# Reordering the front of a fused attention and feed-forward kernel: early masks, later transposes, shared weighing of V, one AV head behind each score tile

## The chip, the cores and the metric

The kernel runs on one core of one Trainium2 chip. Times are device microseconds (us) of one execution. Most executions of a kernel agree within 0.3%; the change concerns about 1%, so the comparisons below use several runs and a 95% interval. A run carries its mean granted TensorE clock (1.0 is full speed). Runs called slow (over 1.5% above the fastest of the same kernel) are left out of the ratios; the medians are over all runs, slow ones too.

## The reference

Batch 8, 8 heads, 576 positions, head size 64: forgetting attention (the scores carry a decay that is the difference of two running sums of log f), followed by a feed-forward layer with exact GELU over the 512 joined head columns.

```python
scores = scale * np.matmul(q, k.transpose(0, 1, 3, 2))
cum    = np.cumsum(np.log(np.clip(f, 0.0001, 1.0)), axis=-1)
scores = np.where(causal, -1e9, scores + cum[:, :, :, None] - cum[:, :, None, :])
attn   = softmax(scores)                      # row maximum taken off, 1e-9 in the sum
x      = (attn @ v).transpose(0, 2, 1, 3).reshape(4608, 512)
h      = x @ w_in                             # 512 x 2048
out    = (0.5 * h * (1 + erf(h / sqrt(2)))) @ w_out
```

## The kernel before

Eight batches go through the same pipeline: attention of batch b is woven into the feed-forward matmuls of batch b-1. For the first batch there is nothing to weave into. That stretch, written out by hand, is the *front*, the first 25 us, and the change touches only it.

The decay is split: the factor that belongs to a query cancels in the softmax, and the factor of a key, exp(-cum), is multiplied into V and into a 65th column of V that yields the sum. This multiplication is the *weighing*. Four *pairs* of heads are numbered 0 to 3; `scores(0, i, t)` is one of four score tiles of pair i with its exponential on ScalarE; `attend_head(i, h)` is an *AV head*, 15 matmuls and a normalization on VectorE.

```python
def weigh_v(b, i, eng=nc.gpsimd):             # V of one pair times exp(-cum)
    ...
    eng.tensor_tensor(vw_of[b][:, hs, :, 0:D], v_sb[:, hs, :, :],
                      w.unsqueeze(3).to_broadcast([P, 2, NBLK, D]), Alu.mult)
    eng.tensor_copy(vw_of[b][:, hs, :, D], w)

def transposes_first(b, i, which, pool, tag): # q or k of one pair on TensorE
    ...                                       # 12 transposes into ps, then ONE copy:
    op = nc.scalar.copy if b == i == which == 0 else nc.vector.tensor_copy
    op((qT, kT)[which][i]..., ps...)

def first_attention():
    ...                                       # pairs 0 and 1
    scores(0, 1, 0)
    transposes(2, m_psum, "m")
    scores(0, 1, 1)
    scores(0, 1, 2)
    transposes(3, m_psum, "m")
    scores(0, 1, 3)
    weigh_v(0, 0, nc.vector)
    gate = x_pool.tile([P, 1], FP32, tag="gate", name="gate")
    nc.gpsimd.tensor_copy(gate[D:P], v_sb[D:P, 0, 4, 0:1])   # holds GpSimd until V is there
    load_w_in(0)
    weigh_v(0, 1)
    load_w_in(1)
    weigh_v(0, 2)
    weigh_v(0, 3)
    ...                                       # loads of the next batch
    scores(0, 2, 0); scores(0, 2, 1); scores(0, 2, 2); scores(0, 2, 3)
    attend_head(0, 0)
    scores(0, 3, 0)
    attend_head(0, 1)
    scores(0, 3, 1)
    ...                                       # the other heads, three to_xT
    gemm1_begin(0, both)                      # first feed-forward matmuls
```

Ahead of this, GpSimd's order of loads and masks: q and k of pairs 0 and 1, an identity, q and k of pair 2, V (issued by SyncE), then two masks (`key_of`, `after`), each a memset and a select on GpSimd, then q and k of pair 3. In the traces each engine works through its own list in the order written here (the kernel has a manual schedule). So whatever stands in front of an instruction in its engine's list delays it, needed or not.

The softmax here doesn't subtract the row's maximum and nothing guards it: scores larger than these inputs give would overflow.

## Time and profile before

| | before |
|---|---|
| median of the runs with the changed kernel | 345.62 us (345.02 to 345.96, 4 runs) |
| span of the profiled run, mean clock | 343.4 us, 0.999 |
| first score exponential | 8.43 us |
| AV head (0,0) starts | 17.36 us |
| first feed-forward matmul ("front's end") | 24.50 us |

These three moments are the yardstick for the front, and the prediction shows the chain of waits that leads to them. Two more lines are needed later. The first is from the table of stretches (window; length; busy us and instructions of TensorE, its weight loads, VectorE, ScalarE, GpSimd; granted clock; DMA share; GB/s), for the sparsest stretch of the front. The second is from GpSimd's timeline: the select that makes a mask.

```profile
15.04:18.46 3.42, 2.30 (x49) 1.56 (x47) 1.47 (x5) 3.34 (x5) 3.05 (x6) 1.00 0.58 84
```

```profile
7.13 0.40 POOL L141 TENSOR_SCALAR_AFFINE_SELECT after<-after 64x256 bf16<-64x256 bf16 x1
```

TensorE is busy 2.30 of 3.42 us (67%) where ScalarE paces, and the clock stays at 1.00. The select takes 0.40 us; VectorE beside it copies keys out of PSUM until 7.26 and a mask from 7.29 on.

### The profile page before, as it was taken

The numbers are of one execution on the slowest core, as the hardware profiler recorded it, in microseconds if no ns is written. First come the engines' busy times: TensorE is split into PE (matmuls) and PEld (weight loads), VectorE is DVE, ScalarE is ACT, GpSimd is POOL, SyncE is SP. The second block draws the span as 40 slices with busy tenths as digits, with TensorE's granted clock in tenths as the row PEclk, the third lists the DMA queues.
The fourth block names the chain that finished last, engine by engine and source line by source line (L and its number), as shares of the span: only waits on it lengthen the run. The fifth ranks groups of instructions, "written<-read, shape, count | busy, mean of one in ns | idle before, by whom it ended". The sixth has DMA issues, their size and how long they took to land.

```text
span 343.4 us, 7895 instructions
## 1 busy us (share of the span) xinstructions
PE 328.6 (96%) x3182; PEld 174.7 (51%) x3227; DVE 187.0 (54%) x424; ACT 212.3 (62%) x296; POOL 124.2 (36%) x256
## 2 busy tenths in 40 slices
PE   7799999999999999999999999999999999999995
PEld 3574555445554456545654565446544654444443
DVE  5660355933467935796479646974597542020011
ACT  5986786773644787368746874687468755504600
POOL 8390672228328034543445243714261430000000
PEclk9999999999999999999999999999999999999999
DMA  8999999989993999578945896499900230011013
GB/s 117 178 176 194 201 166 153 170 158 148 237 184 102 139 192 188 82 101 165 211 121 73 141 212 139 71 160 198 169 31 2 65 88 31 2 61 61 0 38 87
DMA packets 99924, 43.03 MB, mean 125 GB/s; under 512 B 78704, under 2 KB 95344, under 8 KB 99888
## 3 DMA queue, kind: packets, MB, share of 16 engines
q1 hardware_dynamic: 82592, 28.37, 41.4%
q0 software_dynamic: 16896, 13.63, 27.2%
q8 instruction: 25, 0.41, 0.5%
q10 hardware_dynamic: 400, 0.52, 0.4%
q14 instruction: 11, 0.09, 0.1%
HBM read 36.85 MB, written 9.44 MB: 135 GB/s over the span
## 4 chain that ended last, share of the span: by engine, by line
PE 89%; issue 2%; POOL 2%; DVE 2%; ACT 2%; DMA 2%; POOLq 0%; ACTq 0%; DVEq 0%
PE ps L375 36%; PE ps L466 25%; PE o L320 9%; PE ps L408 8%; PE s L289 7%; PE ps L501 2%; ACT e L299 2%; DMA k<-in_k_dram 2%; PE ps_x L353 1%; DVE x L334 1%; POOL q L107 1%; PE ps_f L206 1%; POOL k L107 1%; DVE r L333 0%; DVE xT L356 0%
## 5 line engine op out<-in xcount | busy, mean ns | idle before, releaser
L392 ACT ACTIVATE g<-ps 128x512 bf16<-128x512 f32 x144 | 85.3, 597 | 81.1 <-PE ps L375 81.1
L299 ACT ACTIVATE e<-s 128x896 bf16<-128x896 f32 (+2 forms) x128 | 101.2, 836 | 28.5 <-PE s L289 26.8
L375 PE MATMUL ps<-xT,w_in_sb 128*128 128x512 bf16 x497 | 111.4, 379 | 0.8
L466 PE MATMUL ps<-w_out_sb,g 64*128 64x512 bf16 (+1 forms) x731 | 103.0, 376 | 0.8 <-issue 0.8
L375 PEld LDWEIGHTS <-w_in_sb 128*128 128x128 bf16 x576 | 56.0, 98 | 67.5 <-issue 1.8
L301 POOL TENSOR_SCALAR_AFFINE_SELECT e<-e 128x256 bf16<-128x256 bf16 (+1 forms) x135 | 49.2, 383 | 98.9 <-ACT e L299 98.6
L466 PEld LDWEIGHTS <-g 64*128 64x128 bf16 (+1 forms) x756 | 41.5, 94 | 40.4 <-issue 11.9
L244 DVE COPY qT<-tq 64x288 bf16<-64x288 bf16 x96 | 48.7, 507 | 1.4
L289 PE MATMUL s<-qT,kT 64*128 64x320 bf16 (+4 forms) x384 | 45.8, 276 | 3.6 <-ACT e L299 2.7
L260 POOL TENSOR_TENSOR vw<-v_sb,wT 128x640 bf16<-128x640 f32 x31 | 39.6, 1278 | 23.5 <-DMA v_sb<-in_v_dram 23.3
L320 PE MATMUL o<-vw,e 128*128 128x65 bf16 x960 | 36.8, 194 | 3.5 <-issue 2.4
L474 DVE COPY ot<-ps 128x512 f32<-128x512 f32 x26 | 17.9, 689 | 37.1 <-PE ps L466 35.2
L320 PEld LDWEIGHTS <-e 128*128 128x128 bf16 x960 | 34.8, 98 | 5.3 <-PE ps_x L353 0.3
L244 DVE COPY kT<-tk 64x288 bf16<-64x288 bf16 x96 | 33.0, 343 | 1.6
L334 DVE TENSOR_TENSOR x<-o,r 128x320 bf16<-128x320 f32 x64 | 31.4, 491 | 2.4 <-DVE r L333 0.2
L417 DVE COPY ot<-ps 128x512 f32<-128x512 f32 (+2 forms) x9 | 5.7, 632 | 48.8 <-PE ps L408 31.9
L289 PEld LDWEIGHTS <-kT 64*128 64x128 bf16 x384 | 19.5, 94 | 23.2 <-issue 9.7
L408 PE MATMUL ps<-w_out_sb,g 128*128 128x512 bf16 (+2 forms) x142 | 27.9, 355 | 0.1
L333 DVE RECIPROCAL r<-o 128x5 f32<-128x5 f32 x64 | 12.1, 189 | 27.6 <-PE o L320 27.5
L408 PEld LDWEIGHTS <-g 128*128 128x128 bf16 x144 | 13.5, 98 | 14.5
L476 DVE TENSOR_TENSOR ot<-ot,ps 128x512 f32<-128x512 f32 x26 | 17.9, 687 | 1.5
L365 POOL COPY tails<-xT 128x256 bf16<-128x256 bf16 x8 | 3.2, 399 | 31.3 <-DVE xT L356 31.3
(64 smaller groups left out, 158.1 us busy)
## 6 DMA issues: line engine op xcount, KB each, us to landing
out_dram<-ot SPq DMA_DIRECT2D x32, 256.0 KB, 2.3
v_sb<-in_v_dram SPq DMA_DIRECT2D x24, 256.0 KB, 5.3
q<-in_q_dram POOLq DMA_DIRECT2D x6, 576.0 KB, 6.1
k<-in_k_dram POOLq DMA_DIRECT2D x6, 576.0 KB, 8.2
v_sb<-in_v_dram SPq DMA_DIRECT2D x22, 128.0 KB, 5.1
w_in_sb<-in_moe_w_in_dram POOLq DMA_DIRECT2D x4, 512.0 KB, 6.7
w_out_sb<-in_moe_w_out_dram POOLq DMA_DIRECT2D x4, 512.0 KB, 8.4
q<-in_q_dram POOLq DMA_DIRECT2D x4, 144.0 KB, 4.6
```

The source lines that it names most:

```text
L244: nc.vector.tensor_copy(rows[:, odd], src[odd * D : (odd + 1) * D, 2 * i + h].rearrange("d j p -> d p j"),)
L260: eng.tensor_tensor(vw_of[b][:, hs, :, 0:D], v_sb[:, hs, :, :], w.unsqueeze(3).to_broadcast([P, 2, NBLK, D]), Alu.mult,)
L289: nc.tensor.matmul(to, *ab, start=half < 0, stop=half == 1 or not masked)
L299: nc.scalar.activation(et[:, :, z:c], st[:, :, z:c], Act.Exp, scale=scale)
L301: nc.gpsimd.affine_select(out=et[:, :, c0 + z : c0 + P], in_=et[:, :, c0 + z : c0 + P], compare_op=Alu.is_ge, fill=0.0, base=z, pattern=[[ ...
L320: nc.tensor.matmul(o[:, m, :], e_of[b, i, t][:, h, c : c + P], vw_of[b][:, 2 * i + h, n, :], start=(n == 0), stop=(n == m),)
L334: nc.vector.tensor_tensor(x_of[b, i][:, :, h, :], o[:, :, 0:D], r.unsqueeze(2).to_broadcast([P, NBLK, D]), Alu.mult,)
L375: nc.tensor.matmul(ps, w_in_sb[:, kt, ffb * P : (ffb + 1) * P], src[:, kt, 0:TC], start=(kt == 0), stop=(kt == n_dm - 1),)
L392: nc.scalar.activation(g_of[c][ffb], ps, Act.Gelu)
L408: nc.tensor.matmul(pss[ts][:, c0:c1], g_of[c][kt][:, ts * P : (ts + 1) * P], w_out_sb[:, kt, c0:c1], start=(kt == 0), stop=(kt == n_ff - 1),)
L466: nc.tensor.matmul(banks[r], g_of[c][kt][rows, ts * P : (ts + 1) * P], w_out_sb[rows, kt, :], start=kt == (steps.index("r") if r else 0), ...
L474: nc.vector.tensor_copy(ot, banks[1])
```

## The change

The intent: have the masks ready earlier, take the last key load out of the way of ScalarE's exponentials, relieve GpSimd of half the weighing, and spread the AV heads so that fewer are left when the exponentials end.

```diff
@@ order of loads and masks
+    warm = ...; nc.vector.memset(warm, 0.0)                 # moved up
     load_qk_tokens(0, 0, 2); load_qk_tokens(0, 2, 4); make_identity(nc, ident_bf)
-    load_qk_tokens(0, 4, 6)
-    nc.gpsimd.memset(v_sb[:, :, 0, 0:1], 0.0)
-    load_v(0, 0, 4)
     for t, op, fill in ((key_of, ...), (after, ...)):
-        nc.gpsimd.memset(t[0:D], 0.0)
+        nc.vector.memset(t[0:D], 0.0)
         nc.gpsimd.affine_select(...)
+    nc.gpsimd.memset(v_sb[:, :, 0, 0:1], 0.0)
+    load_v(0, 0, 4)
+    load_qk_tokens(0, 4, 6)
@@ first_attention
     transposes(0, o_psum, "o")
+    nc.scalar.activation(wk, cum, Act.Exp, ...)             # was ahead of transposes(0)
     ...
+    nc.vector.tensor_copy(vw(0)[:, :, :, D], ...)           # one cast in place of four
     scores(0, 1, 2)
-    transposes(3, m_psum, "m")
     scores(0, 1, 3)
-    weigh_v(0, 0, nc.vector)
-    nc.gpsimd.tensor_copy(gate[D:P], v_sb[D:P, 0, 4, 0:1])
+    nc.gpsimd.tensor_copy(gate, v_sb[:, 0, 3, 0:1])
     load_w_in(0); weigh_v(0, 1); load_w_in(1)
-    weigh_v(0, 2)
     weigh_v(0, 3)
+    scores(0, 2, 0)
+    scores(0, 2, 1)
+    transposes(3, m_psum, "m")
+    weigh_v(0, 0, nc.vector)
+    scores(0, 2, 2)
+    attend_head(0, 0)
+    scores(0, 2, 3)
+    attend_head(0, 1)
+    weigh_v(0, 2, nc.vector)
     ...                                  # loads of the next batch
-    scores(0, 2, 0) ... scores(0, 2, 3)  # and heads (0,0), (0,1), ... behind them
+    scores(0, 3, 0); attend_head(1, 0); scores(0, 3, 1); attend_head(1, 1)
+    scores(0, 3, 2); attend_head(2, 0); scores(0, 3, 3); ...
```

More of the change, by code (lines that the diff above doesn't have):

```diff
@@ L122, in load_v @@
             )
+    warm = consts.tile([P, TC], BF16)
+    nc.vector.memset(warm, 0.0)
     f_sb = consts.tile([BH, S], FP32)
@@ L180 @@
     wk = f_sb
-    warm = consts.tile([P, TC], BF16)
-    nc.vector.memset(warm, 0.0)
     nc.vector.memset(ones, 1.0)
@@ L188 @@
     nc.vector.tensor_tensor_scan(cum, ones, lf, 0.0, Alu.mult, Alu.add)
-    nc.scalar.activation(wk, cum, Act.Exp, bias=cum[:, S // 2 : S // 2 + 1], scale=-1.0)
     def warm_up(n):
@@ L251, with vw, weigh_v @@
     vw_of = {}
-    def weigh_v(b, i, eng=nc.gpsimd):
+    def vw(b):
         if b not in vw_of:
             vw_of[b] = v_pool.tile([P, H, NBLK, D + 1], BF16, tag="vw", name=f"vw{b}")
+        return vw_of[b]
+    def weigh_v(b, i, eng=nc.gpsimd):
         hs = slice(2 * i, 2 * i + 2)
@@ L260, in weigh_v @@
         eng.tensor_tensor(
-            vw_of[b][:, hs, :, 0:D],
+            vw(b)[:, hs, :, 0:D],
             v_sb[:, hs, :, :],
@@ L265, in weigh_v @@
         )
-        eng.tensor_copy(vw_of[b][:, hs, :, D], w)
+        if b:
+            eng.tensor_copy(vw(b)[:, hs, :, D], w)
     e_of = {}
@@ L539, in first_attention @@
         transposes(0, o_psum, "o")
+        nc.scalar.activation(
+            wk, cum, Act.Exp, bias=cum[:, S // 2 : S // 2 + 1], scale=-1.0
+        )
         nc.vector.tensor_copy(key_of[D:P], key_of[0:D])
@@ L554, in first_attention @@
         nc.vector.tensor_copy(wT[D:P, 4, :], psw[D:P, 4, :])
+        nc.vector.tensor_copy(
+            vw(0)[:, :, :, D], wT[:, :, 0:H].rearrange("p n h -> p h n")
+        )
         scores(0, 1, 0)
@@ L575, in first_attention @@
         load_qk_tokens(1, 4, 8)
-        scores(0, 2, 0)
-        scores(0, 2, 1)
-        scores(0, 2, 2)
-        scores(0, 2, 3)
-        attend_head(0, 0)
         scores(0, 3, 0)
-        attend_head(0, 1)
+        attend_head(1, 0)
         scores(0, 3, 1)
-        attend_head(1, 0)
+        attend_head(1, 1)
         scores(0, 3, 2)
-        attend_head(1, 1)
+        attend_head(2, 0)
         scores(0, 3, 3)
         to_xT(0, 0, nc.vector.tensor_copy)
-        attend_head(2, 0)
         attend_head(2, 1)
```

## The prediction

> **What bounds the kernel now.** First the page: span, busy shares, the chain that ended last.
>
> ```profile
> span 343.4 us, 7895 instructions
> PE 328.6 (96%) x3182; PEld 174.7 (51%) x3227; DVE 187.0 (54%) x424; ACT 212.3 (62%) x296; POOL 124.2 (36%) x256
> PE 89%; issue 2%; POOL 2%; DVE 2%; ACT 2%; DMA 2%; POOLq 0%; ACTq 0%; DVEq 0%
> ```
>
> TensorE makes up 89% of the chain. The non-TensorE shares sit mostly at the start, the only place the change touches, so I read the chain for the first 30 us (start, length, what; the gaps are mine):
>
> ```profile
> 8.15 5.64 DMA k<-in_k_dram
> 13.84 0.56 PE ps_f L206 x12
> 14.39 0.35 PE s L289 x6
> 14.76 2.22 ACT e L299 x3
> ...
> 17.03 0.40 PE s L289 x6
> 17.43 0.58 PE o L320 x15
> 18.01 0.47 PE s L289 x12
> 18.47 0.58 PE o L320 x15
> ...
> 23.97 0.47 PE o L320 x15
> 24.45 0.05 issue
> 24.50 0.81 PE ps L375 x3
> ```
>
> Three stretches. Up to 13.8 us the last key load decides, because its 24 transposes stand in TensorE's order in front of a score tile. From 14.8 to 17.0 ScalarE's exponentials (L299) pace. From 17.0 to 24.5 TensorE alternates score tiles (0.30 to 0.47 us) and AV heads (15 matmuls, 0.58 us) nearly without a gap. The first feed-forward matmul (L375) stands at 24.50; call this the front's end. After it the chain is matmul after matmul to about 38 us and nothing in it waits for a DMA, so I take a shift of the front's end to pass 1:1 into the total.
>
> Then VectorE's timeline and GpSimd's (start, length, instruction, idle before):
>
> ```profile
> 13.43 0.76 DVE L213 COPY qT<-ps_f 128x576 bf16<-128x576 bf16 x1
> 14.43 0.76 DVE L213 COPY kT<-ps_f 128x576 bf16<-128x576 bf16 x1 [0.25 <-PE ps_f L206]
> 15.11 0.82 DVE L260 TENSOR_TENSOR vw<-v_sb,wT 128x640 bf16<-128x640 f32 x1
> 18.04 0.20 DVE L333 RECIPROCAL r<-o 128x5 f32<-128x5 f32 x1 [1.92 <-PE o L320]
> ```
>
> ```profile
> 14.88 0.19 POOL L563 COPY gate<-v_sb 64x1 f32<-64x1 f32 x1 [4.94 <-DMA v_sb<-in_v_dram]
> 16.21 1.27 POOL L260 TENSOR_TENSOR vw<-v_sb,wT 128x640 bf16<-128x640 f32 x1
> 18.41 1.29 POOL L260 TENSOR_TENSOR vw<-v_sb,wT 128x640 bf16<-128x640 f32 x1
> 19.80 1.28 POOL L260 TENSOR_TENSOR vw<-v_sb,wT 128x640 bf16<-128x640 f32 x1
> ```
>
> The reader is to see that the first weighing of V (VectorE) is finished at 15.9, long before the first AV head asks for it at 17.4: now nobody waits for it. Finally two VectorE timelines from later, for the same kind of copy (SBUF to SBUF): four of them alone, and four while GpSimd weighs.
>
> ```profile
> 61.52 1.45 DVE L244 COPY kT<-tk 64x288 bf16<-64x288 bf16 x4
> ```
>
> ```profile
> 142.74 5.04 DVE L244 COPY qT<-tq 64x288 bf16<-64x288 bf16 x4
> ```
>
> **What the Trainium skill says.** "GPSIMD Engine Reference", section 8 (Key points): GpSimd shares its SBUF interfaces with VectorE, with contention for VectorE instructions in a 2-port mode or with two SBUF inputs. The trace agrees strongly for the copies: alone, four take 1.45 us together (0.32 each in the single records); the second row's three that lie under a GpSimd weighing of 1.27 take 1.45 each, as 14 do in the whole trace, and the weighing isn't slowed. For a VectorE weighing (two SBUF inputs) no overlap occurs in this trace. The same page, 4.1 (Engine selection), puts GpSimd at about 2x slower for two-input elementwise work; here 1.28 against 0.82 us, 1.56x. "ScalarE: Activation LUTs", What ACT_TABLE_LOAD costs: about 1283 ns a load plus a drain; the trace has 1.28 us and no drain between (Ln ends 4.74, load 4.76 to 6.05, Exp at 6.16). "TensorE: Matmul & The Clock Gate", What's actually happening: an idle window of about 3.4 us halves the clock; here it stays at 1.00 through the sparse stretch 15.9 to 17.4.
>
> **The change, part by part.**
>
> *Masks early.* Two GpSimd memsets (about 0.25 us each exposed) go to VectorE, which has the room before the f load lands at 3.55. GpSimd's selects are done near 5.5 instead of 7.5. But the score tile waits for the copies of both masks to the upper partitions on VectorE, which stand behind the kT copy (6.50 to 7.26) and end at 7.93 either way. Gain: nothing. The q/k loads of pair 2 are issued 0.9 us later (5.6 and 6.25) and, with about 4.9 us to landing, arrive by 11.3; their transposes come near 11.6 to 12.0. Just in time.
>
> *Exponential of the decay after the qT copy.* The instruction order shows that the table load moves with it: qT copy 6.06 to 6.68, load to 7.96, Exp (0.78) to 8.75, less 0.1 overlap: the first score exponential starts at 8.67 instead of 8.43. Cost 0.24 us; ScalarE paces from here, so it carries.
>
> *Last pair's transposes behind two more score tiles.* This removes the stall at 13.8: ScalarE idled 0.61 there. Stepping on with the recorded spacing of back-to-back exponentials (0.81, 0.69, 0.80, 0.60 for a pair's four tiles) and the gap that stays around pair 2's transposes, exponential (1,3) runs 14.28 to 14.98. Score tile (2,1) takes the freed buffer at 15.03; the transposes follow at 15.33 (0.30 after, as now after the other 6-matmul tile).
>
> *Weighing of pair 0.* In VectorE's new order it still stands behind these transposes' two copies. qT copy at 15.92 (0.59 after the first transpose, as twice before), kT 16.59, weighing 17.27, with 0.82 us to 18.09. AV head (0,0) stands in TensorE's order behind score tile (2,2), which is done near 16.4, and ahead of tile (2,3). So it waits until 18.14, against 17.36 now, and ScalarE starves behind it from about 17.4. The wait for the key load has become a longer wait for a weighing.
>
> *Is the weighing alone on the SBUF?* GpSimd's gate now looks at a V piece landing near 13.5 instead of 14.9, so w_in's first piece is issued at 14.0, weighing (0,1) runs 14.8 to 16.1, issue to 16.9, weighing (0,3) 16.95 to 18.2. It covers VectorE's start at 17.27. If that is blocked as the copies are, it ends near 18.2 + 0.75 = 18.95 and the head starts at 19.0.
>
> *From the first head to the front's end.* TensorE's work there: 8 heads, score tiles (2,3) to (3,3), 3 groups of transposes of x. Adding the recorded lengths in the new order: 8 x 0.58 + 0.33 + 0.47 + 0.30 + 0.38 + 0.33 + 3 x 0.30 = 7.35 us. Now it is 24.50 - 17.36 = 7.14 without tile (2,3), including about 0.2 of gaps. VectorE keeps up: each head costs it 0.71, the weighing (0,2) of 0.82 after head (0,1) ends 0.7 us before it is used. One head fewer after the last exponential helps nothing where TensorE is the limit. So the front ends at 18.14 + 7.35 = 25.5 (alone) or 19.0 + 7.35 = 26.35 (blocked): +1.0 or +1.85 us.
>
> *Casts.* Three GpSimd casts of 0.22 and one on VectorE of 0.29 become one VectorE copy at about 11.3, in idle time: 0 on the path. Loads of w_in and of batch 1's q and k keep their issue times within 1 us (the memset ahead of them now waits for VectorE's weighing (0,2), ending at 21.2 to 22.1; it stands at 21.16 now) and have over 1 us of slack against a later front.
>
> Sum: +0.24 (Exp), -0.6 (stall removed), then a new wait, for a net +1.0 to +1.85 us. Weighting blocked at two to one: 345.62 + 1.6 = about 347.2.
>
> **Rivals.**
> A: the intended gain. Without the wait for the weighing, ScalarE would end its 16 tiles near 21.5 (8.67 + four pairs of 2.9 + gaps) and, with one head fewer behind, the front would end 1.35 us earlier: 344.3. For it: the stall at 13.8 is real. Against it: the orders of VectorE and TensorE, which fix the wait; and TensorE's 7.35 us after that head.
> B: weighing alone on the SBUF, because GpSimd's second weighing starts later than VectorE's or VectorE isn't blocked with two inputs: 346.6. For it: V's second half may land later now that w_in competes with it. Against it: the 1.45 us copies.
> C: pair 2's loads land late (V is now issued ahead of them): another 0.3 to 0.8 us of ScalarE idle near 12. But most of it falls in front of the same wait: up to 348.
> D: TensorE's lull (16.4 to 19.0, 2.6 us) trips the clock gate: a few us at half rate, +1 to +2 us. Against: under the 3.4 us window.
>
> **Range and chances.** Both main branches are slower; A's level needs an error in the orders that I read. Low 345.9 leaves room for half the wait, high 348.4 for C on top of the blocked case. 2% is 6.9 us, five times what is at play in a front of 25 us: faster 0.005, within 0.985, slower 0.01.
>
> **What would show it.** Right: the head (0,0) waiting for VectorE's weighing of V, ScalarE idle over 1.2 us before tile (2,3); that weighing lasting over 1.2 us if blocked, 0.82 if alone; first score exponential at about 8.7; no wait for k; L375's counterpart first at 25.4 to 26.4. Wrong: head (0,0) starting before 17.4, a wait for pair 2's keys over 0.5 us, a granted clock below 1 near 20, or a front shift that the span doesn't repeat.

## The result, and the profile after

The changed kernel takes 348.09 us in the median (347.60 to 348.82, 4 runs) against 345.62. The ratio is 1.0072 [1.0054 to 1.0089]. Within 2%, and slower beyond doubt. The four clocks are 0.988 to 0.995, where the kernel before has 0.999 in its profile. The profiled run is the slowest of the four.

From the page: span, and the clock in 40 slices (in tenths, 9 is full speed).

```profile
span 347.0 us, 7892 instructions
...
PEclk9969999999999999999999999999999999999999
```

The span grew by 347.0 - 343.4 = 3.6 us, and one slice near the front's end has a low clock. The chain of waits through the front (start, length, what; `s` is a score tile, `o` an AV head, `ps` the feed-forward; the line numbers differ by one from the kernel before):

```profile
16.22 0.75 DVE kT L210
16.97 1.24 DVE vw L260
18.20 0.04 issue
18.24 0.98 PE o L321 x15
19.23 0.54 PE s L290 x6
19.77 0.94 PE o L321 x15
...
28.10 0.81 PE ps L376 x3
```

Where the chain before read "ScalarE's exponential, score tile, AV head", two VectorE steps stand: the copy of pair 3's keys, then the weighing of V (`vw`). The head (0,0) starts at 18.24 instead of 17.36, though it uses nothing of pair 3. TensorE's timeline has the wait itself, in brackets:

```profile
18.24 0.98 PE L321 MATMUL o<-vw,e 128*128 128x65 bf16 x15 [2.10 <-DVE vw L260]
```

And the head runs slowly: 0.94 to 0.98 us for the 15 matmuls that took 0.58 before. The front ends at 28.10 instead of 24.50: 3.60 us later, all that the span grew.

VectorE's and GpSimd's timelines give the two weighings and the mask:

```profile
16.88 1.31 DVE L260 TENSOR_TENSOR vw<-v_sb,wT 128x640 bf16<-128x640 f32 x1
```

```profile
4.96 1.45 POOL L138 TENSOR_SCALAR_AFFINE_SELECT after<-after 64x256 bf16<-64x256 bf16 x1
...
6.41 0.68 POOL L107 DMA_DIRECT2D q<-in_q_dram  x1
...
16.21 1.29 POOL L260 TENSOR_TENSOR vw<-v_sb,wT 128x640 bf16<-128x640 f32 x1
```

VectorE's weighing takes 1.31 us instead of 0.82 where GpSimd's of pair 1 overlaps it. The select takes 1.45 us instead of 0.40, because it now lies beside VectorE's running sum (from 4.66, for 1.54 us instead of 1.35), and the q load of pair 2 behind it is issued at 6.41 instead of 4.69.

The table of stretches tells why the heads are slow:

```profile
14.28:17.69 3.41, 1.80 (x48) 1.29 (x43) 2.15 (x3) 2.79 (x4) 2.46 (x4) 1.00 0.68 121
17.69:21.10 3.41, 2.86 (x44) 2.35 (x45) 1.51 (x5) 0.70 (x1) 0.55 (x1) 0.50 1.24 209
21.10:24.52 3.42, 3.42 (x52) 2.41 (x49) 2.42 (x6) 1.73 (x2) 2.85 (x4) 0.50 0.72 118
```

The clock's records stand on a grid of 3.41 us, on which I laid the stretches. In 14.28 to 17.69 TensorE is busy 1.80 us, 53%. In the two stretches that follow the granted clock is 0.50. TensorE's wait for the weighing is 2.1 us (16.16 to 18.24), far less than one stretch; it was enough that 1.53 us of it fell into one. The rest of it, 0.55 us, lies in the next stretch, where TensorE was busy 2.86 us (84%), and the clock stayed at 0.50 for one stretch more.

### The profile page after: what moved, and what is told of

Read it like the earlier page. It is cut to its first block, busy times and chain, and to the rows that moved or that the text cites. A ratio compares the mean times of both kernels' runs of the same rounds, so it can differ in the third digit from the quotient of the medians.

```text
span 347.0 us, 7892 instructions
## 1 busy us (share of the span) xinstructions
PE 330.7 (95%) x3182; PEld 176.1 (51%) x3227; DVE 188.7 (54%) x427; ACT 212.5 (61%) x296; POOL 123.9 (36%) x250
## 4 chain that ended last, share of the span: by engine, by line
PE 91%; ACT 3%; DVE 3%; issue 2%; POOL 0%; ACTq 0%; DVEq 0%
PE ps L376 35%; PE ps L467 25%; PE o L321 9%; PE ps L409 8%; PE s L290 8%; ACT e L300 2%; PE ps L502 2%; PE ps_x L354 1%; PE ps_f L203 1%; PE ps_w L192 1%; DVE x L335 1%; DVE kT L210 0%; ACT L541 0%; DVE vw L260 0%; DVE xT L357 0%
## 5 line engine op out<-in xcount | busy, mean ns | idle before, releaser
L290 PE MATMUL s<-qT,kT 64*128 64x320 bf16 (+4 forms) x384 | 46.7, 280 | 3.7 <-ACT e L300 3.0
L321 PE MATMUL o<-vw,e 128*128 128x65 bf16 x960 | 38.4, 197 | 5.4 <-issue 2.4
L321 PEld LDWEIGHTS <-e 128*128 128x128 bf16 x960 | 36.2, 100 | 7.5 <-issue 2.3
L409 PEld LDWEIGHTS <-g 128*128 128x128 bf16 x144 | 13.5, 98 | 14.5
```

The source lines that it names most:

```text
L290: nc.tensor.matmul(to, *ab, start=half < 0, stop=half == 1 or not masked)
L321: nc.tensor.matmul(o[:, m, :], e_of[b, i, t][:, h, c : c + P], vw_of[b][:, 2 * i + h, n, :], start=(n == 0), stop=(n == m),)
L409: nc.tensor.matmul(pss[ts][:, c0:c1], g_of[c][kt][:, ts * P : (ts + 1) * P], w_out_sb[:, kt, c0:c1], start=(kt == 0), stop=(kt == n_ff - 1),)
```

## The experiments

My theory after this: the loss is the wait for the weighing, which stands behind pair 3's copies on VectorE, plus what the granted clock takes because of it. Rivals: the weighing is merely too slow because GpSimd's lies beside it; the clock is luck and the same with any order; the loss comes from the first part of the change, masks and loads, which I had put at nothing. All kernels below gave correct results. Kernels are compared only within the same rounds.

| run | what it is | median us | ratio to before [95%] | clocks of its runs |
|---|---|---|---|---|
| `e1_filled` | changed, the wait filled with dummy matmuls | 346.96 | 1.0042 [1.0016, 1.0068] | 0.998 to 1.0 |
| `e2_weigh_first` | changed, weighing ahead of the copies | 347.08 | 1.0045 [1.0009, 1.0082] | 0.999 to 1.0 in 4, 0.995 in 2 |
| `e3_alone` | changed, no GpSimd weighing of pair 1 | 348.78 | 1.0084 [1.0056, 1.0113] | 5 at 0.995, one 0.985 |
| `e4_early_masks` | before + masks, loads and Exp of the change | 348.27 | 1.0059 [1.0028, 1.0089] | 0.998 to 0.999 in 3, 0.985 to 0.989 in 3 (one of them slow) |
| `e5_loads_first` | `e4_early_masks`, loads ahead of the masks | 346.11 | 0.9991 [0.9967, 1.0015] | 0.999 to 1.0 |
| `e6_both` | before + transposes later + head order | 346.72 | 1.0024 [0.9989, 1.0058] | 0.998 to 1.0, one 0.995 |
| `e7_av_order` | before + head order | 346.49 | 1.0018 [0.9984, 1.0052] | 1.0, one 0.99 |
| `e8_transposes` | before + transposes later | 346.52 | 1.0006 [0.9977, 1.0035] | 0.998 to 1.0, one 0.995 |
| `e9_gate` | `e6_both`, gate one piece of V earlier | 347.32 | 1.0018 [0.9978, 1.0059] | 0.998 to 1.0, one slow 0.995 |
| `e10_two_back` | changed, loads first and weighing first | 345.70 | 0.9977 [0.9945, 1.0010] | 0.999 to 1.0, one slow 0.995 |
| `e11_again` | the changed kernel once more | 349.73 | 1.0112 [1.0077, 1.0147] | 0.984 to 0.995 in all |
| `e12_loads_back` | changed, loads first only | 347.94 | 1.0065 [1.0052, 1.0078] | 0.993 to 0.995 in 5, 0.999 in 2 |

The first four shared 11 runs of before (345.69 in the median), the next four 11 (345.85), `e9_gate` to `e11_again` 11 (345.77), the last 11 (345.44). The moments of the front in the profiled run of each (us):

| profile | first score exponential | head (0,0) | front's end | end less first exponential |
|---|---|---|---|---|
| before | 8.43 | 17.36 | 24.50 | 16.07 |
| after | 8.32 | 18.24 | 28.10 | 19.78 |
| `e1_filled` | 9.59 | 19.35 | 26.77 | 17.18 |
| `e2_weigh_first` | 9.35 | 17.11 | 27.92 | 18.57 |
| `e3_alone` | 9.60 | 19.04 | 28.01 | 18.41 |
| `e4_early_masks` | 9.23 | 18.42 | 25.56 | 16.33 |
| `e5_loads_first` | 9.14 | 17.61 | 24.76 | 15.62 |
| `e6_both` | 8.37 | 16.16 | 23.71 | 15.34 |
| `e7_av_order` | 8.62 | 16.82 | 24.66 | 16.04 |
| `e8_transposes` | 8.21 | 16.56 | 24.23 | 16.02 |
| `e9_gate` | 9.03 | 16.82 | 24.04 | 15.01 |
| `e10_two_back` | 9.60 | 17.36 | 24.96 | 15.36 |
| `e11_again` | 9.11 | 19.14 | 27.68 | 18.57 |
| `e12_loads_back` | 9.30 | 18.73 | 27.28 | 17.98 |

The first exponential wanders between 8.2 and 9.6 from profile to profile, mostly because TensorE starts slowly, and the clock's records begin, at 1.00, at a different moment each time: at 4.04 us in the changed kernel's profile, where the first eleven matmuls take 3.90 us, at 7.12 in `e3_alone`, where the same eleven take 4.88. (In `e4_early_masks`, with 4.19, it was the first q and k that landed late, at 5.96 and 6.70 instead of 4.57 and 5.86.) So I compare the last column, which takes this out.

### `e1_filled`: the wait kept, TensorE kept busy

```diff
         scores(0, 2, 2)
+        warm_up(8)               # eight matmuls whose result nobody reads
         attend_head(0, 0)
```

> The changed kernel with 8 idle matmuls (about 0.22 us each) put into TensorE's wait in front of AV head (0,0). Clock theory: more than half of the loss is the granted clock falling to 0.50 because TensorE has nothing to do for 2.1 us; then head (0,0) still starts near 18.2 us, the clock stays 1.00, the front ends near 25.6 instead of 28.1, and the time falls from 348.1 to about 346.7. Rival (the wait and the blocked weighing are the whole loss, the clock falls for another reason): the time stays at 348 within 0.4.

All six clocks stayed at 0.998 or above and the time fell to +0.42%, which splits the loss into wait and clock. In the chain the dummies stand where the wait was, and the head behind them runs at full speed; the stretch shows TensorE at 92%.

```profile
18.06 1.46 PE ps_w L192 x6
19.51 0.47 PE o L321 x15
```

```profile
17.02:20.43 3.41, 3.14 (x41) 1.93 (x42) 2.33 (x5) 1.43 (x3) 3.07 (x3) 1.00 1.11 168
```

From the last column of the table: after less filled is 19.78 - 17.18 = 2.6 us, the clock's part in the changed kernel's profile; filled less before is 1.1 us, the wait's. The split is rough: in this profile GpSimd's weighing had ended before VectorE's began, which took 0.82 us and not 1.31, and the dummies held the head until 19.35, 0.37 us after that weighing. From the head to the front's end, which leaves all this out, it took 7.42 us against 9.86: 2.4 us of clock. The idea that the clock is luck falls: all ten runs of the changed kernel (with `e11_again`) have 0.995 or less, and none of these six. But the kernel before is not free of it: 2 of its 44 runs beside the experiments have 0.993 and 0.990.

### `e2_weigh_first`: the wait taken away

```diff
         scores(0, 2, 1)
+        weigh_v(0, 0, nc.vector)
         transposes(3, m_psum, "m")
-        weigh_v(0, 0, nc.vector)
         scores(0, 2, 2)
```

> The changed kernel with VectorE's weighing of pair 0 put ahead of the two copies of the last pair's transposes. Order theory: the wait of 2.1 us disappears, head (0,0) starts near 16.4, the clock stays 1.00; if nothing else waits the front ends near 23.8 and the time is about 344.9. But the second half of V lands only at 21.3 in the changed kernel, and VectorE's weighing of pair 2 needs it: if that becomes the next wait, head (2,0) starts near 22.1, the front ends near 25.6 and the time is about 346.6. Rival (order is not the cause): time stays near 348.

The wait for this weighing is gone, head (0,0) starts at 17.11, but the time is still +0.45%. Two of the six runs have a low clock, the profiled one among them, and one with a full clock took 348.09 us, which no trace explains. In the profile another wait took its place, at the fifth head, as the expectation had allowed for:

```profile
14.62 6.78 DMA v_sb<-in_v_dram
...
21.57 0.83 DVE vw L260
...
23.09 0.84 PE o L321 x15
```

A piece of V's second half is issued at 14.62 and lands at 21.40. The weighing of pair 2, now on VectorE and ahead of the head's normalization there, waits for it; head (2,0) starts after a wait of 2.12 us. TensorE is busy 1.29 us of the stretch 19.91 to 23.32 (38%), and in the next the clock is at 0.50. How late that piece lands differs: at 18.18 in `e3_alone` and 18.35 in `e1_filled`, which have the same order of loads. So the second wait need not come in every run. The theory "one wait" was too small: a second one lay hidden behind the first.

### `e3_alone`: VectorE's weighing with nothing beside it

```diff
-        weigh_v(0, 1)                        # GpSimd
         load_w_in(1)
         ...
         weigh_v(0, 0, nc.vector)
+        weigh_v(0, 1, nc.vector)
```

> The changed kernel with pair 1 weighed on VectorE too, behind pair 0, so that GpSimd weighs nothing beside VectorE's weighing of pair 0. Sharing theory: that weighing takes 0.82 us instead of 1.31, head (0,0) starts near 17.75 instead of 18.24; TensorE's wait is then 1.6 us and may be short enough for the clock to hold: front's end near 25.5 and time about 346.6. If the clock still falls, time about 347.6. Rival (1.31 us is not from sharing): weighing stays at 1.3 us and the time at 348.

The first weighing took its 0.82 us alone, yet TensorE still waited 1.61 us, the clock fell in all six runs, and nothing was gained (+0.84%). The contention moved on: GpSimd's next weighing lay beside VectorE's second, which took 1.90 us. The "merely too slow" rival falls. `e11_again` agrees: there the first weighing took 0.82 us unhindered, and the head waited 1.6 us all the same. The place in the queue costs, not the speed.

### `e4_early_masks` and `e5_loads_first`: the first part of the change alone

```diff
@@ e4_early_masks: the kernel before, with
+    masks' memsets on VectorE; the masks ahead of load_qk_tokens(0, 4, 6) and load_v(0, 0, 4)
+    the decay's Exp behind transposes(0); the memset of `warm` moved up
@@ e5_loads_first: e4_early_masks, with
+    load_qk_tokens(0, 4, 6), the memset of v_sb and load_v(0, 0, 4) ahead of the masks again
```

> The kernel before with only the first part of the change: masks and memsets early, order of loads, exponential of the decay behind the qT copy. By the prediction this part gains nothing and costs 0.24 us. By the trace of the changed kernel the first score exponential is not later, but the select for the second mask lies under VectorE's scan and takes 1.45 us, so pair 2's and 3's keys are issued later and the last key lands near 14.9 instead of 13.8: score tile (1,3) would wait 1.1 us more and the time be about 346.7. Rival (this part is harmless): 345.6.

> As the early-masks experiment, but the loads of q and k of pair 2 and of V are issued before the masks are made, as in the kernel before (VectorE still clears the masks, the exponential of the decay still comes later). Collision theory: what hurt was the select lying under VectorE's scan in front of these issues; then the selects take 0.40 us each again, the last key lands near 13.6, and the time is 345.6 within 0.4. Rival (the later exponential, or the cleared masks on VectorE, cost it): time stays at 347 or more.

By itself this part costs 0.59%, and putting the loads back in front takes it all away (0.9991). In the profile of `e4_early_masks` the last key load lands at 14.85 (13.79 before), TensorE waits 0.58 us for it (0.45 before), and the front stretches by 0.26 us (last column); more of that profile's loss, 1.7 us, lies in a later stage (see `e6_both`). GpSimd's timeline of `e5_loads_first` shows the other half: the select, now after VectorE's running sum, is short again, and the load stands ahead of it.

```profile
4.62 0.66 POOL L107 DMA_DIRECT2D q<-in_q_dram  x1
...
6.32 0.41 POOL L141 TENSOR_SCALAR_AFFINE_SELECT after<-after 64x256 bf16<-64x256 bf16 x1
```

The last key lands at 13.12 there. I cannot split the 0.59% of the timed runs between front and later stages, as only one run of each kernel left a trace; half of `e4_early_masks`' runs also had a clock of 0.985 to 0.989, while its profiled run had none of that: its sparsest stretch kept the clock at 61% busy.

```profile
14.43:17.85 3.42, 2.07 (x42) 1.39 (x43) 2.27 (x4) 2.54 (x4) 1.82 (x3) 1.00 0.77 143
```

### `e6_both`, `e7_av_order`, `e8_transposes`: the parts that ought to gain

Each is the kernel before with only the later place of `transposes(3)`, only the new order of AV heads, or both; the weighing of pair 0 stays early, behind `scores(0, 1, 3)`.

```diff
@@ e8_transposes (and e6_both)
-        transposes(3, m_psum, "m")           # behind scores(0, 1, 2)
         ...
         scores(0, 2, 1)
+        transposes(3, m_psum, "m")
@@ e7_av_order (and e6_both)
         scores(0, 2, 2)
+        attend_head(0, 0)
         scores(0, 2, 3)
+        attend_head(0, 1)
         ...                                  # and so on, one behind each tile
@@ e6_both only
-        load_w_in(1); weigh_v(0, 2)
+        weigh_v(0, 2); load_w_in(1)
```

> The kernel before with the two parts that should gain, without what hurt: the last pair's transposes behind two more score tiles, and one AV head behind each score tile from (2,2) on; VectorE's weighing of pair 0 stays ahead of the transposes' copies, the masks and loads stay as before, and GpSimd weighs pair 2 before it issues the second piece of w_in. Order theory: head (0,0) near 16.4 us, clock 1.00, no wait over 0.5 us after it, front's end near 23.8, time about 344.9. Rival (the front is limited elsewhere, by the last key or by GpSimd's weighings): 345.6.

> The kernel before with only the order of the AV heads changed: one behind each score tile from (2,2) on. The heads come 0.6 us earlier, but GpSimd's weighing of pair 2 ends at 21.1 and head (2,0) would ask for it near 20.5; so a new wait of about 0.5 us takes the place of the gain: front's end 24.5 within 0.3, time 345.6 within 0.4. Rival (the order alone pays): front's end 24.0, time 345.1.

> The kernel before with only the last pair's transposes moved behind score tile (2,1). ScalarE's stall of 0.6 us at 14.2 goes; no wait for the last key. The heads still begin behind tile (2,3), about 0.5 us earlier; head (2,0) may wait 0.2 us for GpSimd's weighing. Front's end near 24.1, time about 345.2. Rival (the transposes' copies come too late for score tile (3,0), or the stall was not on the path): 345.6 or more.

In the profile `e6_both` shortens the front as intended, to 23.71 (0.8 us less). The total shows none of it: 1.0024, and `e7_av_order` and `e8_transposes` are level as well. What the front gained was given back 50 us later. The chain of `e6_both` in the third batch's stage has what the kernel before does not have there, a wait for a V load and GpSimd's weighings behind it:

```profile
71.99 3.68 DMA v_sb<-in_v_dram
...
75.84 1.28 POOL vw L260
...
84.73 0.97 PE o L320 x25
```

I timed the stages, one per batch, by the loads of ScalarE's tables, two per batch. That stage takes 25.05 us in the kernel before and in after, and more where the last V load of the third batch lands late, counted from the front's end:

| profile | last V of the third batch lands, from the front's end | stage |
|---|---|---|
| after | 49.97 | 25.05 |
| before | 50.52 | 25.05 |
| `e10_two_back` | 50.71 | 25.05 |
| `e7_av_order` | 51.24 | 25.24 |
| `e6_both` | 51.96 | 25.96 |
| `e8_transposes` | 52.14 | 26.14 |
| `e1_filled` | 52.46 | 26.48 |
| `e4_early_masks` | 52.77 | 26.78 |

From about 51.05 on the stage grows by as much as V is late (`e6_both`: 51.96 - 51.05 = 0.91, and 25.96 - 25.05 = 0.91). The kernel before has some 0.5 us of slack there. Counted from the start of the kernel, V landed at 75.0 before and at 75.7 in `e6_both`: the shorter front did not bring the transfer forward, so relative to it V came later. Why V came even 0.65 us later in absolute time, no run settles. This also burdens `e1_filled` (+1.4 us of stage), `e4_early_masks` (+1.7) and `e3_alone` (+0.55), on top of their fronts.

### `e9_gate`: the loads moved along

`e6_both` with the gate on an earlier piece of V, so that w_in is issued at 14.29 instead of 15.9.

```diff
-        nc.gpsimd.tensor_copy(gate[D:P], v_sb[D:P, 0, 4, 0:1])
+        nc.gpsimd.tensor_copy(gate, v_sb[:, 0, 3, 0:1])
```

> The combined kernel (transposes later, heads earlier) with GpSimd's gate looking at the fourth V piece instead of the fifth, so that w_in's first piece is issued about 1.3 us earlier and the DMA queues do not run empty near 16 us. Give-back theory: the combined kernel's front is 0.8 us shorter, but the third batch's stage then waits for its V, whose last piece lands a fixed time after the DMA stream and not after the front (stage 25.96 instead of 25.05 us); with the stream 1 us earlier that V lands within 51.0 us of the front's end, the stage is 25.05 to 25.3 and the time 345.0. Rival (the longer stage is chance, or the front's gain is not real): time as the combined kernel's, 346.5.

In its profile the V load lands 51.19 us after the front's end, at the edge of the slack, and the stage is back at 25.05; that run, 344.99 us, is its fastest. But the median of its runs is 347.32, two of the fast ones 348.06 and 348.72 with clocks of 1.0 and 0.998, and the ratio (1.0018) includes 1. The traced run supports the mechanism; that the gate secures it is not shown.

### `e10_two_back`, `e11_again` and `e12_loads_back`: what the whole loss consists of

`e10_two_back` is the changed kernel with two orders put back, and nothing else: the loads of pair 2 and V ahead of the masks, the weighing of pair 0 ahead of pair 3's copies. `e12_loads_back` puts back the first of them alone (`e2_weigh_first` is the second alone), and `e11_again` repeats the changed kernel.

```diff
@@ e10_two_back and e12_loads_back: ahead of the masks
+    load_qk_tokens(0, 4, 6)
+    nc.gpsimd.memset(v_sb[:, :, 0, 0:1], 0.0)
+    load_v(0, 0, 4)
@@ e10_two_back only
+        weigh_v(0, 0, nc.vector)
         transposes(3, m_psum, "m")
-        weigh_v(0, 0, nc.vector)
```

> The changed kernel with two things put back: the loads of pair 2 and V issued before the masks, and VectorE's weighing of pair 0 ahead of the last pair's copies. If these two orders are the whole cause of the loss, no wait of TensorE over 1 us is left in the front, the clock stays 1.00, the front ends near 24.2 and the time is 345.3 to 346.0, no slower than the kernel before. Rival (another part of the change costs time, as sharing the weighing): 347 or more.

> The changed kernel itself, once more beside the others on the same chip. If the fall of the granted clock belongs to the kernel and not to chance, every run has a mean clock of 0.988 to 0.995 and the time is 347.6 to 348.8; if it was chance, some runs have 0.999 or more and about 346.8.

> The changed kernel with only the order of the loads put back (loads of pair 2 and of V ahead of the masks); the weighing of pair 0 still stands behind the copies of pair 3. With the two orders put back the loss was gone (345.70); with the weighing alone put back it was 347.08 (+0.45%). Theory, the two orders add up: the wait stays, head (0,0) starts 0.5 to 1.5 us later than its 17.4 of the kernel with both put back, TensorE waits over 1 us for the weighing of V on VectorE, and the clock drops in one or two windows in part of the runs: median 346.5 to 347.5 (+0.2 to +0.5%), runs with the full clock near 346, with 0.995 near 347.5. Rival, the loads are the whole loss and the wait is free once V and the keys come early: 345.7 +- 0.4 and full clock in all runs. Rival two, the wait is the whole loss: 348 or more as in the changed kernel, clock 0.995 in nearly all runs.

The four corners, each against its own runs of before: neither put back +1.12% (and +0.72% earlier), weighing alone +0.45%, loads alone +0.65%, both -0.23% with an interval that holds 0. So neither order is the whole loss, and within the noise the two together are: 345.70 against 349.73 on one chip. In the profile of `e10_two_back`, head (0,0) follows its score tile at 17.36 with no wait, and TensorE works on to the front's end at full clock.

My expectation for `e12_loads_back` (346.5 to 347.5) was 0.4 us too low at its upper end: its wait remained, at 1.61 us, five of seven runs lost clock, and in its profile later stages lost 2.4 us as well (the last V landed 53.65 us after the front's end, the stage took 26.94). Its two runs with a full clock, 347.47 and 347.94, have no trace; what they lost beyond the wait stays open.

`e11_again` and `e12_loads_back` also give the clearest lines for the clock. Three stretches in a row of `e11_again`:

```profile
12.47:15.88 3.41, 2.08 (x45) 1.44 (x43) 1.52 (x2) 2.69 (x4) 0.28 (x2) 1.00 1.06 201
15.88:19.29 3.41, 1.74 (x46) 1.27 (x41) 2.16 (x3) 2.58 (x4) 2.74 (x3) 1.00 0.70 124
19.29:22.70 3.41, 3.41 (x57) 2.76 (x55) 1.81 (x5) 1.05 (x2) 1.27 (x1) 0.50 1.19 180
```

And of `e12_loads_back`:

```profile
16.34:19.75 3.41, 1.80 (x48) 1.41 (x43) 2.47 (x5) 1.75 (x4) 1.16 (x2) 1.00 1.10 169
19.75:23.16 3.41, 3.41 (x56) 2.70 (x55) 2.86 (x6) 1.93 (x3) 1.38 (x2) 0.50 1.06 167
```

A stretch at 61% is followed by one at full clock, a stretch at 51% or 53% by one at half. Over all traces here: 67% (before), 61% (`e4_early_masks`, `e11_again`) and 60% (`e12_loads_back`, 2.04 us of 88.01 to 91.42) kept it; 53% (after, `e3_alone`, `e12_loads_back`), 51% (`e11_again`) and 38% (`e2_weigh_first`) lost it. Where between 53% and 60% it turns, no run tells. Once at half, the clock was back after one stretch at 91% (`e3_alone`) or 100% (`e2_weigh_first`, `e11_again`, `e12_loads_back`), and not after the 84% of the changed kernel.

No version is shown to beat the kernel before. `e10_two_back` is the best of them, at 0.9977 with an interval up to 1.0010.

## Why the prediction was right or wrong

The predicted time, 347.2 us, was 0.9 us below the measured 348.09, which lies in the range and within 2%, slower as foretold. The repeat, at 349.73, would have lain above the range: the size was less certain than the range said. Point by point:

- **The wait for the weighing: right.** The head waits for VectorE's weighing of V, 2.1 us, and starts at 18.24; the prediction had 18.14 for a weighing alone and 19.0 for a blocked one. The chain in front of it was summed almost exactly: from the first score exponential to the weighing's start 16.88 - 8.32 = 8.56 us, predicted 17.27 - 8.67 = 8.60. ScalarE idles 2.71 us before tile (2,3)'s exponential, where over 1.2 was foretold. `e2_weigh_first` shows the wait gone with the order.
- **The weighing beside GpSimd: right in kind, a term mis-sized.** Blocked, yes, but 1.31 us, so 0.49 above the 0.82 alone, where 0.86 was in the sum. It was the weighing of pair 1, not of pair 3: the gate came at 15.16, not at 13.5 to 14, since V came later. And `e3_alone` shows that the blocking decided nothing.
- **The clock: the step that failed.** Rival D was set aside with "under the 3.4 us window". That compared the length of the wait with the length of a window. What the records show is a share: a wait of 1.6 to 2.1 us that leaves TensorE 51% to 53% busy within one stretch of the grid is enough. The wait of 16.16 to 18.24 straddled a border of the grid, and two stretches were at half clock in the profiled run. From the head to the front's end it took 28.10 - 18.24 = 9.86 us where the prediction summed 7.35: 2.5 us of clock, in line with the 2.4 to 2.6 us that `e1_filled` took away. Runs at 0.995 lost one stretch (3.41 x 0.5 / 346 = 0.5%), so about half of that, an estimate from the clocks. Added to the prediction's unblocked branch (346.6), 1.25 to 2.5 us more would have given 347.9 to 349.1.
- **"Masks early: gain nothing", at a cost of 0: half right.** It gained nothing, but alone it costs 0.59% (`e4_early_masks`). The term missed: the select was taken at its 0.40 us while it moved under a VectorE instruction with two SBUF inputs, where it takes 1.45. The loads of pair 2 were issued at 6.41 rather than 5.6. The keys of pair 2 still came in time (landed 11.39, predicted 11.3), so rival C did not occur at the place it named. What came late was V's second half: 21.26 instead of 16.61, hidden behind the first wait until `e2_weigh_first` uncovered it. The masks are not its only cause: in `e12_loads_back`, with the loads first, it landed at 20.55, right beside a w_in load that the earlier gate had let go at 14.66.
- **Exp behind the qT copy, +0.24 us: not settled.** The order on ScalarE came out as foretold (copy ends 6.33, table load, Exp from 7.64, first score exponential on its heels), and from the copy's end to that exponential it took 8.32 - 6.33 = 1.99 us, as predicted (8.67 - 6.68). But the copy ended 0.35 us earlier than assumed, and so the exponential stood at 8.32. The slow start moves it by more than the term itself.
- **A shift of the front passes 1:1 into the span: right for this pair** (3.60 us against 3.6), and the stages behind are equal. The companion step, loads with "over 1 us of slack", held only because the front ended later. In the other direction the slack is 0.5 us, and `e6_both` shows a shorter front not reaching the total. By that slack rival A's 344.3 would have fallen short too (an estimate: no run of it).

Two terms that were low or zero (clock 2.5, masks) and two that were high (blocked weighing by 0.37, Exp by up to 0.24) partly offset each other: that the time fell into the range was in part luck, the wait that makes it slower was not.

## What to carry to other kernels

Before moving work in an in-order queue, look at what then stands in front of the producer that someone else needs: here a copy for pair 3 stood in front of the weighing for pair 0, and loads stood behind masks. Judge a new TensorE wait by the busy share of the whole clock stretch that it falls into, not by its own length, and if it cannot be removed, fill it: dummy matmuls kept the clock. And a front that ends earlier pays only if the transfers that later stages wait for move with it.

## What the Trainium skill lacked or had wrong

- "TensorE: Matmul & The Clock Gate", What's actually happening, says in its table that the clock goes cold after at least one idle window of about 3.4 us. The length of the window and its being free-running agree (records on a grid of 3.41 us, which lies differently in each profile). But the window need not be idle: the clock fell to 0.50 after stretches in which TensorE was 51% to 53% busy, and held after 60% to 67%. The page gives no such share.
- "GPSIMD Engine Reference", section 8 (Key points), names the contention with VectorE instructions of two SBUF inputs, without a size. The runs give sizes, for both engines: VectorE's weighing 1.31, 1.48 and 1.90 us instead of 0.82 where GpSimd's had begun before it; GpSimd's select 1.45 instead of 0.40 and its weighing 1.92 instead of 1.28 where VectorE's had begun before. Mostly the one that began first kept its speed, with one exception: in `e10_two_back` VectorE's weighing began 0.37 us ahead of GpSimd's and took 2.36 us.
- "ScalarE: Activation LUTs", What ACT_TABLE_LOAD costs, adds a drain of about 1380 ns to each load. Here none is seen after the change either: the copy ends at 6.33, the load runs 6.34 to 7.62, Exp starts at 7.64.
- "DMA: Bandwidth & Descriptors", Issuing engines are not separate DMA queues, says that transfers from different issuing engines interleave on the same 16 DMA engines. The runs are in keeping with it, and show what it may cost a small load: the last piece of V, issued by SyncE at 13.50, lands after 3.1 us in the kernel before; issued at 14.76, 0.63 us ahead of GpSimd's w_in, it takes 6.5 us (lands 21.26). It is not so each time: in `e1_filled`, issued at 15.00 and 0.72 us ahead of w_in, it took 3.35 us; what makes the difference, no run settles. The section has no number for this.
